# Weight splits held in order, the second pair's norms in later units, the last down products done plainly: one block of attention and GLU on one core

## The chip, the cores and the metric

The kernel runs on one core of a Trainium2 chip. The time is that of one execution on the device, in microseconds (us); the kernel before was run three times: 3179.58, 3184.73 and 3190.97, median 3184.73. PE is the matrix engine (TensorE), DVE the vector engine, ACT the scalar engine, POOL GpSimd, and SP the engine that issues all transfers (DMAs) here. Each engine runs its own instructions in order.

## The reference

All tensors are float32; S = 2048 rows, D = 576, 32 query heads over 16 key heads of 128, of whose cached 2048 keys the last W = 512 are used, and F = 4608.

```python
mod = (silu(c) @ w_mod).reshape(1, 6, 1, 576)
sa, ca, ga, sb, cb, gb = mod[:, 0], ..., mod[:, 5]
h = layernorm(x) * (1 + ca) + sa
q = (h @ wq) by heads; k, v = caches[:, :, Sk - W:], each for two query heads
x = x + ga * ((softmax(q @ k.T * 128**-0.5) @ v) by rows @ wo)
h = layernorm(x) * (1 + cb) + sb
x = x + gb * ((sigmoid(h @ w_gate) * (h @ w_up)) @ w_down)
```

## The kernel before

Products are made from split operands: a float32 number is a high part `hi` (a copy, rounded, made by ACT) and a low part `lo` (what is left, a subtraction on POOL or DVE), and `three` (L237) gives the three matmuls lo*hi, hi*lo, hi*hi.

The rows are four blocks of 512 in two halves: blocks 0 and 1 go through all heads first, then blocks 2 and 3, 128 (block, head) pairs, each in four steps (512 steps n). A step issues, in program order, a quarter of a coming query projection (`qproj`), the scores of step n + 2 (`scores`), the transposes of the probabilities (`transp`), one half of a row tile's output projection (`wo_acc`), a quarter of probabilities times values (`pv`) and the other half of `wo_acc`. The softmax of a step is a maximum on DVE (L354), an exponential on ACT (L356), four transposes on PE (L367) and two evictions (L370, L371).

What has to be made beside the steps is put in a table: `at_n(n, fn, ...)` calls fn at step n, in program order. wq is loaded 16 steps ahead of its use and split 8 ahead (`split_a`: ACT L207, POOL L208 and L209, four buffers wa), wo is loaded (L225), scaled by the gate (L420) and split (`split_b`: ACT L230, POOL L232, two buffers wb). Keys are loaded 15 steps ahead of their first step (L309) and transposed by PE 7 ahead (L315). The loads of wq, wo, keys and values share four buffers named raw.

The GLU of the second part is done by a seven-product scheme (Strassen-Winograd) over two halves of D, a pair of row blocks and pairs of F tiles. Its weights are prepared during attention as 135 *chunks*: each is loaded, summed, split and stored to DRAM (wsc for gate and up, dsc for down) while the other half's rows are at rest; the spare rows' buffers (x0, x1, or x2, x3) hold it. Chunk k starts at a step `n`, the next one three steps later, and takes its parts at fixed distances; sums alternate between two places by k, hi between two, raw between three. Chunks run from step 4 and, for the second part, from step 300 on. A chunk of kind tail is stored by 48 small DMAs (L648), the others by four or five (L654, L656).

A scheduler that goes by its own costs may move any instruction ahead of others on its engine, unless it is pinned: `keep_in_program_order` keeps pinned instructions in program order among themselves. The chunks are pinned and so is the copy in `split_b`; loads of raw and the splits of wq are not.

After attention, the second part runs 72 units u (pair of blocks, F tile). A unit makes the seven products (`product`, L849) of row combinations (hc, made by `load_combo` from transposed rows ts, loaded L723, transposed L736, split L737 and L739) with weights sw (L759); within each product two *down groups* (three matmuls, L241, and an addition to an accumulator in SBUF, L832 or L834) of the pair of F tiles before are done. A pair of units gives seven down values times four row tiles, 28 groups. After the last group of a pair of blocks, `finish` combines the accumulators by eight additions for each row tile and stores the output. The rows of the first pair are normed during attention (`early_norm`, `early_sums`); those of the second pair in units 0 to 2 (`late_stats`, then `late_tile`: L507 to L523), and the block buffers x2, x3 are parked in DRAM before (L536). The junction in what follows is the time from the last step of attention to the first full units, the pair switch is where blocks 2 and 3 take over.

## Time and profile before

| what | value |
|---|---|
| runs | 3179.58, 3184.73, 3190.97 us; median 3184.73 |
| profiled execution | 3187.44 us, its span 3185.7, granted clock 0.983 |
| PE busy | 3077.7 us, 17000 matmuls |
| DVE, ACT, POOL busy | 2173.0, 1444.2, 1555.8 us |
| DMA | 499.96 MB, mean 157 GB/s |
| attention | to 1880 us |
| junction | 1880 to 2000 us |
| GLU units | to 3150 us |
| last groups and stores | 3150 to 3186 us |

A row of the timeline reads: start, length, engine, line, operation, result <- operands, shape, count, and in brackets how long the engine stood idle just before and what ended it. The page's span is what one core did; the time on the device is 1.7 us longer.

### The profile page before, as it was taken

The page shows a single profiled execution, that of the slowest core. Times are in us where ns is not written, and L with a number is a line of the kernel's source. Part 1 is how long each engine was busy: PE and PEld are TensorE (multiplying, and loading weights), DVE is VectorE, ACT ScalarE, POOL GpSimd, SP SyncE. Part 2 cuts the span into 40 slices and gives each one's busy share as a digit, 9 for nine tenths or more (in the row PEclk, how much of TensorE's full clock was granted, in tenths as well). Part 3 has the DMA queues.
Part 4 walks back from the last instruction along what each step waited for, and adds up shares of the span by engine and source line. Part 5 has one row for each costly group of instructions (what it writes and reads, how often), then busy time and mean ns, then how long its engine had stood idle before and what let it go on. Part 6 is the DMA issues. An engine that isn't in the chain of part 4 may idle for free.

```text
span 3185.7 us, 50897 instructions
## 1 busy us (share of the span) xinstructions
PE 3077.7 (97%) x17000; PEld 2659.9 (83%) x17000; DVE 2173.0 (68%) x4214; ACT 1444.2 (45%) x3189; POOL 1555.8 (49%) x1925
## 2 busy tenths in 40 slices
PE   8999999999999999999999977999999999999998
PEld 6888887888888888888888866888888888888887
DVE  7777776777888777777777785555555665555556
ACT  5665655655554555656555532322222322222322
POOL 3656555664344335756565413433434353443435
PEclk8999999999999999999999988999999999999998
DMA  5556566555303235544444338766666776666663
GB/s 159 152 154 167 141 159 164 157 156 140 119 30 97 66 99 145 142 105 124 107 123 111 81 109 272 227 199 199 200 197 200 222 245 201 200 198 200 197 200 115
DMA packets 574437, 499.96 MB, mean 157 GB/s; under 512 B 191840, under 2 KB 455008, under 8 KB 573152
## 3 DMA queue, kind: packets, MB, share of 16 engines
q1 hardware_dynamic: 574176, 496.72, 54.4%
q8 instruction: 135, 2.21, 0.3%
q14 instruction: 126, 1.03, 0.1%
HBM read 356.35 MB, written 140.18 MB: 156 GB/s over the span
## 4 chain that ended last, share of the span: by engine, by line
PE 86%; POOL 4%; DVE 3%; DMA 3%; issue 2%; SPq 1%; ACT 1%; POOLq 0%; DVEq 0%; ACTq 0%
PE a L849 14%; PE w L241 12%; PE wo L241 11%; PE qp L241 11%; PE ot L241 10%; PE st L241 10%; PE c L849 7%; PE st L367 6%; PE b L849 3%; POOL x L637 1%; SPq L523 0%; PE w L736 0%; DMA ts<-scr 0%; DMA sw<-wsc 0%; DMA scr<-x 0%
## 5 line engine op out<-in xcount | busy, mean ns | idle before, releaser
L834 DVE TENSOR_TENSOR x<-w,x 128x288 f32<-128x288 f32 x976 | 443.2, 457 | 484.4 <-PE w L241 481.9
L241 PE MATMUL wo<-wb,ov 128*128 128x288 f32 x3072 | 623.1, 311 | 3.8 <-DVE ov L385 2.1
L241 PEld LDWEIGHTS w<-sd,hl 128*128 128x128 f32 x3024 | 515.0, 191 | 106.8 <-DVE x L832 12.1
L849 PE MATMUL a<-hc,sw 128*128 128x512 f32 x2016 | 582.4, 394 | 10.3 <-DVE hc L739 9.8
L241 PE MATMUL w<-sd,hl 128*128 128x288 f32 x3024 | 564.8, 297 | 20.5 <-DVE x L832 11.8
L370 ACT ACTIVATE ptt<-st 128x512 fp32r<-128x512 f32 x512 | 305.8, 597 | 606.5 <-PE st L367 605.9
L394 DVE SCALAR_TENSOR_TENSOR x<-wo,rs,x 128x288 f32<-128x288 f32 x1024 | 513.8, 512 | 55.7 <-PE wo L241 5.6
L354 DVE TENSOR_REDUCE neg<-st 128x1 f32<-128x512 f32 x512 | 352.6, 689 | 288.6 <-PE st L241 286.0
L241 PEld LDWEIGHTS wo<-wb,ov 128*128 128x128 f32 x3072 | 486.7, 190 | 56.0 <-DVE ov L385 4.9
L241 PE MATMUL qp<-hTm,wa 128*128 128x512 f32 x1536 | 445.5, 399 | 4.9 <-DVE qt L338 4.6
L241 PE MATMUL ot<-ptt,vs 128*128 128x512 f32 x1536 | 446.9, 399 | 0.0
L241 PE MATMUL st<-kt,qt 128*128 128x512 f32 x1536 | 440.1, 395 | 3.3 <-DVE ptt L371 3.2
L849 PEld LDWEIGHTS a<-hc,sw 128*128 128x128 f32 x2016 | 355.9, 188 | 49.4 <-DVE hc L739 10.3
L371 DVE TENSOR_TENSOR ptt<-st,ptt 128x512 fp32r<-128x512 f32 x512 | 348.7, 681 | 44.7 <-ACT ptt L370 44.4
L356 ACT ACTIVATE pp<-st,neg 128x512 f32<-128x512 f32 x512 | 350.4, 684 | 42.6 <-DVE neg L354 40.4
L241 PEld LDWEIGHTS st<-kt,qt 128*128 128x128 f32 x1536 | 289.0, 189 | 66.7 <-DVE ptt L371 3.9
L367 PEld LDWEIGHTS st<-ident,pp 128*128 128x128 f32 x2048 | 255.1, 140 | 97.9 <-ACT pp L356 30.8
L367 PE MATMUL st<-ident,pp 128*128 128x128 f32 x2048 | 308.8, 273 | 25.1 <-ACT pp L356 25.0
L849 PE MATMUL c<-hc,sw 128*128 128x512 f32 x1008 | 302.9, 395 | 7.0 <-DMA sw<-wsc 3.8
L637 POOL TENSOR_TENSOR x<-x,x 128x96 fp32r<-128x96 f32 (+3 forms) x364 | 228.3, 645 | 130.0 <-ACT x L632 126.4
L241 PEld LDWEIGHTS qp<-hTm,wa 128*128 128x128 f32 x1536 | 263.1, 190 | 31.5 <-DVE qt L338 5.6
L241 PEld LDWEIGHTS ot<-ptt,vs 128*128 128x128 f32 x1536 | 262.2, 190 | 23.6 <-DVE ptt L371 0.2
(140 smaller groups left out, 3710.8 us busy)
## 6 DMA issues: line engine op xcount, KB each, us to landing
sw<-wsc SPq DMA_DIRECT2D x504, 320.0 KB, 3.2
sd<-dsc SPq DMA_DIRECT2D x252, 288.0 KB, 2.8
wsc<-x SPq DMA_DIRECT2D x72, 448.0 KB, 3.4
raw<-in_A_wo_dram SPq DMA_DIRECT2D x64, 288.0 KB, 3.0
wsc<-x SPq DMA_DIRECT2D x72, 256.0 KB, 3.3
dsc<-x SPq DMA_DIRECT2D x54, 336.0 KB, 3.1
raw<-in_A_wq_dram SPq DMA_DIRECT2D x64, 256.0 KB, 3.0
dsc<-x SPq DMA_DIRECT2D x162, 96.0 KB, 2.5
```

What stands on the lines that cost most here:

```text
L241: nc.tensor.matmul(p, l, r, start=first and n == 0, stop=last and n == len(pairs) - 1)
L354: nc.vector.tensor_reduce(NEG[b][:, i : i + 1], p, axis=AX.X, op=OP.max, negate=True)
L356: nc.scalar.activation(PP[n], p, AF.Exp, bias=NEG[b][:, i : i + 1], accum_out=SUM[b][:, i : i + 1])
L367: nc.tensor.transpose(p[:, k * P : (k + 1) * P], PP[n][:, k * P : (k + 1) * P], ident)
L370: nc.scalar.activation(PT[b][:, 0, :, cols], pv_, AF.Copy)
L371: nc.vector.tensor_sub(PT[b][:, 1, :, cols], pv_, f32(PT[b][:, 0, :, cols]))
L394: nc.vector.scalar_tensor_tensor(xv, p, RS[b][:, i : i + 1], xv, op0=OP.mult, op1=OP.add)
L637: pin(nc.gpsimd.tensor_sub(v.bitcast(F32R), v, hi[:, a:b, :]))
L834: nc.vector.tensor_add(acc, p, acc)
L849: nc.tensor.matmul(p, l, r, start=first and n == 0, stop=n == len(pairs) - 1, skip_group_check=not first)
```

## The change

In attention, the high parts of wq and wo are pinned at their step, and the low parts become steps of their own two steps later, pinned too (so a raw buffer is freed later); wo's scaling is pinned. A chunk's sums come 3 steps after its load instead of 4, its copies 7 instead of 6, its subtractions 8 instead of 7 and its store 9 instead of 8. Then the rows: x2 and x3 are parked at the end of unit 0, after `late_stats`, which stands there now pinned; `late_tile` moves to units 4, 9, 14 and 19, reads the parked rows back into ts buffers and stores the seven combinations with 28 DMAs for a tile instead of 16. The loads of ts (`stage`) run two combinations ahead. At the end, the last pair of F tiles (group GL) is not summed by the seven-product scheme: its four values are multiplied by four of the eight plain quarter weights, 32 down groups instead of 28, as soon as each value is there, added to accumulators that the pair before (group 34) has already combined, in units 70 and 71 with three or six groups in a product. For that dsc of the last group has an eighth row.

```diff
-    def split_a(raw):
+    def split_a_hi(raw):
         sp = wp.tile([P, 2 * NC + 1, P], F32R, tag="wa", name="wa", bufs=4)
-        nc.scalar.activation(sp[:, : NC + 1, :], raw, AF.Copy)
-        nc.gpsimd.tensor_sub(sp[:, NC + 1 :, :], raw[:, :NC, :], f32(sp[:, :NC, :]))
-        nc.gpsimd.tensor_sub(sp[TAIL:, NC, :], raw[TAIL:, NC, :], f32(sp[TAIL:, NC, :]))
+        pin(nc.scalar.activation(sp[:, : NC + 1, :], raw, AF.Copy))
         return sp
+
+    def split_a_lo(raw, sp):
+        pin(nc.gpsimd.tensor_sub(sp[:, NC + 1 :, :], raw[:, :NC, :], f32(sp[:, :NC, :])))
+        pin(nc.gpsimd.tensor_sub(sp[TAIL:, NC, :], raw[TAIL:, NC, :], f32(sp[TAIL:, NC, :])))
...
     def scale_o(hh):
-        nc.gpsimd.tensor_mul(RB[hh], RB[hh], gate)
+        pin(nc.gpsimd.tensor_mul(RB[hh], RB[hh], gate))
...
         at_n(max(q_first(hh) - 8, NLO + 1), split_q, hh)
+        at_n(max(q_first(hh) - 6, NLO + 1), split_q_lo, hh)
...
         at_n(n, split_o, hh)
+        at_n(min(n + 2, o_first(hh) - 1), split_o_lo, hh)
...
-        at_n(n + 4, bg_sums, k)
-        at_n(n + 6, bg_hi, k)
-        at_n(n + 7, bg_lo, k)
-        at_n(n + 8, bg_store, k)
+        at_n(n + 3, bg_sums, k)
+        at_n(n + 7, bg_hi, k)
+        at_n(n + 8, bg_lo, k)
+        at_n(n + 9, bg_store, k)
...
-    for b in range(HB, NB):
-        park_x(b)
...
+    def late_tile(t):
+        lo, hi = slice(0, D2), slice(D2, D)
+        h0, h1, ts_ = [fh.tile([P, 2, D3], F32, tag="ts", name=n, bufs=3).rearrange("p a d -> p (a d)")[:, :D]
+                       for n in ("h0", "h1", "tt")]
+        for i, h in enumerate((h0, h1)):
+            nc.sync.dma_start(h, xscr[HB + i][:, t, :])
...
-        if u == 0:
-            late_stats()
-            late_tile(0)
-        if u == 1:
-            late_tile(1)
-            late_tile(2)
-        if u == 2:
-            late_tile(3)
-            init_acc(0)
...
+        if u in (4, 9, 14, 19):
+            late_tile((u - 4) // 5)
+        if u == NF - 2:
+            stage(1, 0)
...
+        downs = {U - 2: (0, 1, 2, 3, 4, 5), U - 1: (1, 3, 5)}.get(u, (2, 5))
...
+            if g == GL:
+                a, ops = (A11, ((0, A12), (7, S4))) if u % 2 else (A12, ((1, A12), (4, S4)))
+                VAL[g, a] = v
+                split_val(g, a)
+                todo += [(g, (a, o, to), t) for t in range(TPB) for o, to in ops]
```

**SP at a key load of the second run of chunks, near step 354** (raw_15798 and raw_15769 are those keys; raw_15841 and raw_15810 the wo rows that follow; dsc is a chunk's store; what a row waits for stands in brackets). Before:

```order
L202 DMA raw_15794<-in_A_wq_dram 64x128 [waits DMAHW5_49]
L309 DMA raw_15798<-in_A_k_cache_dram 128x512
L654 DMA dsc1_305<-x1_110 896x1x96 [waits DMAHW7_49,Activation_49]
L656 DMA dsc1_305<-x0_109 128x2x96 [waits DMAHW0_49,Pool_49]
L656 DMA dsc1_305<-x1_110 128x2x96 [waits DMAHW1_49,Pool_49]
L656 DMA dsc1_305<-x0_109 128x96 [waits DMAHW2_49,Pool_49]
L656 DMA dsc1_305<-x1_110 128x2x96 [waits DMAHW3_49,Pool_49]
L225 DMA raw_15841<-in_A_wo_dram 128x576 [waits DMAHW4_49]
L588 DMA x0_109<-in_B_w_down_dram 128x96 [waits DMAHW5_49,DMAHW0_49]
```

Now:

```order
L204 DMA raw_15765<-in_A_wq_dram 64x128 [waits DMAHW4_49]
L317 DMA raw_15769<-in_A_k_cache_dram 128x512
L232 DMA raw_15810<-in_A_wo_dram 128x576 [waits DMAHW6_49,DMAHW5_49,PE_49]
L670 DMA dsc1_305<-x1_110 128x7x96 [waits DMAHW7_49,Activation_49]
L672 DMA dsc1_305<-x0_109 128x2x96 [waits DMAHW0_49,Pool_49]
L672 DMA dsc1_305<-x0_109 128x2x96 [waits DMAHW1_49,Pool_49]
L672 DMA dsc1_305<-x0_109 128x96 [waits DMAHW2_49,Pool_49]
L672 DMA dsc1_305<-x0_109 128x2x96 [waits DMAHW3_49,Pool_49]
L602 DMA x0_109<-in_B_w_down_dram 128x96 [waits DMAHW4_49,DMAHW0_49]
```

The load of wo now stands ahead of the chunk's store, in the row behind the key load, and waits for PE: it reuses the buffer that holds those keys (the program's addresses of the two are the same).

**POOL and PE at the same place.** On POOL, now (x0 is the chunk's place; its first sum waits for a DMA, the store of two chunks before, and wa_15763 and wb_15771 are the low parts of wq and wo):

```order
L625 TENSOR_TENSOR x0_109<-x0_109 128x96 [waits DMAHW1_49,Pool_49]
L626 TENSOR_TENSOR x0_109<-x0_109 128x96 [waits Pool_49]
L627 TENSOR_TENSOR x0_109<-x0_109 128x96 [waits DMAHW3_49]
L628 TENSOR_TENSOR x0_109<-x0_109 128x96 [waits Pool_49]
L216 TENSOR_TENSOR wa_15763<-raw_15405,wa_15763 128x512
L217 TENSOR_TENSOR wa_15763<-raw_15405,wa_15763 64x128 [waits Pool_49]
L241 TENSOR_TENSOR wb_15771<-raw_15467,wb_15771 128x576 [waits PE_49,Pool_49]
```

PE before (st<-ident,raw are the key transposes, pp those of the probabilities):

```order
L367 MATMUL st_16116<-ident_69,pp_16033 128x128 x4
L241 MATMUL wo_16123<-wb_15800,ov_16085 128x288 x3
L241 MATMUL ot_16128<-ptt_15946,vs_15661 128x512 x3
L241 MATMUL wo_16132<-wb_15800,ov_16085 128x288 x3
L315 MATMUL st_16145<-ident_69,raw_15798 128x128 x4
L241 MATMUL qp_16166<-hTm_10987,wa_15790 128x512 x3
L241 MATMUL st_16170<-kt_15444,qt_15936 128x512 x3
L367 MATMUL st_16179<-ident_69,pp_16068 128x128 x4
```

PE now:

```order
L375 MATMUL st_16095<-ident_69,pp_16006 128x128 x4
L249 MATMUL ot_16107<-ptt_15918,vs_15634 128x512 x3
L323 MATMUL st_16122<-ident_69,raw_15769 128x128 x4
L249 MATMUL qp_16136<-hTm_10967,wa_15763 128x512
L249 MATMUL ot_16107<-ptt_15918,vs_15634 128x512 x2
L249 MATMUL st_16140<-kt_15414,qt_15908 128x512 x3
L375 MATMUL st_16149<-ident_69,pp_16040 128x128 x4
L249 MATMUL ot_16107<-ptt_15918,vs_15634 128x512 x2
L249 MATMUL st_16179<-kt_15414,qt_16084 128x512 x3
```

The wo groups of this step are gone from it (they stand four steps later, behind the query rows that read wa_15763), and only one query row is left before the subtractions.

**SP at the end of attention** (xscr2 and xscr3 are the parked rows of blocks 2 and 3). Before:

```order
L536 DMA xscr2_266<-x2_111 128x2304
L723 DMA ts_22716<-scr0_262 128x768
L536 DMA xscr3_267<-x3_112 128x2304
L759 DMA sw_22710<-wsc0_268 128x640
L759 DMA sw_22712<-wsc0_268 128x640
L759 DMA sw_22714<-wsc0_268 128x640
L723 DMA ts_22718<-scr0_262 128x768
```

Now:

```order
L553 DMA xscr2_266<-x2_111 128x2304
L736 DMA ts_22717<-scr0_262 128x768
L736 DMA ts_22719<-scr0_262 128x768
L736 DMA ts_22721<-scr0_262 128x768
L770 DMA sw_22777<-wsc0_268 128x640
L736 DMA ts_22723<-scr0_262 128x768
```

Three loads of ts stand right behind the parking of x2, and the parking of x3 is some 35 rows further on.

More of the change, by code (lines that the diff above doesn't have):

```diff
@@ L550, in adaln_block_kernel @@
     wsc = [dram.tile([P, 7, 5, P], F32, tag=f"wsc{f}", name=f"wsc{f}") for f in range(NF)]
-    dsc = [dram.tile([P, 7, 2, D2], F32, tag=f"dsc{g}", name=f"dsc{g}") for g in range(NF // 2)]
+    dsc = [dram.tile([P, 8, 2, D2], F32, tag=f"dsc{g}", name=f"dsc{g}") for g in range(NF // 2)]
     DW = D2 // 3
@@ L727, in load_combo @@
     def load_combo(pair, c):
-        if (pair, c) not in STG:
-            stage(pair, c)
         halves = STG.pop((pair, c))
@@ L771, in adaln_block_kernel @@
     x22 = bg_view(3, TPB * D2, [TPB, D2])
[L772 removed]
+    GL = 2 * NG - 1
+    sd_uses = [(g, a) for g in range(GL) for a in ORDER] + [(GL, i) for i in (0, 7, 1, 4)]
     at_sd = [0]
@@ L816, in finish, with down @@
         nc.gpsimd.tensor_add(c[S1], c[S1], c[S3])
-        for a, b, n0 in ((A12, b0, 0), (A22, b1, 0), (S4, b0, D2), (S1, b1, D2)):
-            nc.sync.dma_start(of[b][:, t, n0 : n0 + D2], c[a])
+        if pair == 0:
+            for a in (A12, A22, S4, S1):
+                store_out(a, pair, t)
+    def down(a, t, hl, w, fresh):
+        cols = slice(t * P, (t + 1) * P)
+        p = fpsum("w", 4, [P, D2])
+        mm_seq(p, three(hl[:, 0, cols], hl[:, 1, cols], w[:, 0, :], w[:, 1, :]))
+        acc = ACC[a][:, t, :]
+        if fresh:
+            nc.vector.tensor_copy(acc, p)
+        else:
+            nc.vector.tensor_add(acc, p, acc)
     def down_some(k):
@@ L950, in adaln_block_kernel @@
         nc.vector.tensor_mul(v1, v1, g1)
+        if u == 0:
+            late_stats()
         g = u // 2
-        if u % 2 == 0:
+        if g == GL:
+            a, ops = (A22, ((1, A22), (4, S1))) if u % 2 else (A21, ((0, A22), (7, S1)))
+            VAL[g, a] = v1
+            split_val(g, a)
+            todo += [(g, (a, o, to), t) for t in range(TPB) for o, to in ops]
+        elif u % 2 == 0:
             VAL[g, A21] = v1
```

138 lines of the change are left out of this document (84 added, 54 removed).

## The prediction

> **What bounds the kernel now.** I read the page first, then PE's waits, then busy time by stage, then single stretches. The page:
>
> ```profile
> PE 3077.7 (97%) x17000; PEld 2659.9 (83%) x17000; DVE 2173.0 (68%) x4214; ACT 1444.2 (45%) x3189; POOL 1555.8 (49%) x1925
> ```
>
> PE (TensorE) is busy 97% of the span, so an edit pays only where PE stands, or where it runs at a lower granted clock. PE's waits, largest first:
>
> ```profile
> PE st L367 <- ACT pp L356: 25.0, 11, 4.7
> PE w L241 <- DVE x L832: 11.8, 1, 11.8
> PE w L736 <- DMA ts<-scr: 11.8, 5, 8.5
> PE a L849 <- DVE hc L739: 9.8, 1, 9.8
> ...
> PE w L241 <- POOL hl L791: 4.7, 5, 1.7
> ...
> PE c L849 <- DMA sw<-wsc: 3.8, 1, 3.8
> ...
> PE st L241 <- DVE ptt L371: 3.2, 1, 3.2
> ```
>
> Columns: total us, times, longest. The next view is busy time by window (start:end, length, PE, PEld, DVE, ACT, POOL, granted clock, DMA share, GB/s; x counts instructions):
>
> ```profile
> 1100.00:1200.00 100.00, 100.00 (x573) 86.63 (x572) 75.79 (x140) 56.36 (x129) 38.77 (x55) 1.00 0.38 99
> 500.00:600.00 100.00, 94.48 (x521) 80.54 (x520) 68.20 (x126) 54.87 (x128) 54.47 (x78) 0.97 0.58 151
> 700.00:800.00 100.00, 96.74 (x543) 83.20 (x542) 71.67 (x132) 57.02 (x133) 58.31 (x85) 0.98 0.56 147
> 1300.00:1400.00 100.00, 96.86 (x545) 83.37 (x544) 71.92 (x132) 58.14 (x145) 64.41 (x112) 0.98 0.46 117
> 1500.00:1600.00 100.00, 96.87 (x544) 83.44 (x543) 72.63 (x134) 56.34 (x144) 57.05 (x101) 0.98 0.41 105
> 1600.00:1700.00 100.00, 97.18 (x546) 83.55 (x545) 71.76 (x131) 57.41 (x147) 66.84 (x120) 0.98 0.49 127
> 1880.00:1900.00 20.00, 1.95 (x7) 1.55 (x8) 15.65 (x45) 1.57 (x3) 10.15 (x8) 0.55 0.66 236
> 1900.00:1920.00 20.00, 18.60 (x106) 14.77 (x105) 10.97 (x18) 11.26 (x20) 0.00 (x0) 0.94 0.81 255
> 1920.00:1940.00 20.00, 15.39 (x68) 12.05 (x67) 12.77 (x17) 5.57 (x11) 8.79 (x7) 0.92 0.88 268
> 1940.00:1960.00 20.00, 8.15 (x37) 6.60 (x36) 10.07 (x13) 4.94 (x9) 15.88 (x12) 0.76 0.69 190
> 1960.00:1980.00 20.00, 18.34 (x89) 16.10 (x89) 8.36 (x18) 4.17 (x7) 3.81 (x3) 0.90 0.86 266
> 1980.00:2000.00 20.00, 19.45 (x97) 16.70 (x97) 10.12 (x22) 5.77 (x10) 8.51 (x7) 0.91 0.91 329
> 2600.00:2700.00 100.00, 100.00 (x543) 87.55 (x542) 56.21 (x114) 29.63 (x51) 41.91 (x33) 1.00 0.68 206
> 3150.00:3186.00 36.00, 21.25 (x102) 17.75 (x100) 24.91 (x52) 2.82 (x5) 25.04 (x24) 0.76 0.25 82
> ```
>
> Undisturbed attention does 573 matmuls in 100 us, the GLU 543. Three places lose time. Attention windows fall short by counts: 521, 543, 545, 544 and 546 against 573 are 9.1 + 5.2 + 4.9 + 5.1 + 4.7 = 29 us. The junction (1880 to 2000) is PE-busy 81.9 of 120 us, 38.1 idle; multiplying each busy time by the missing clock adds 8.8, so 47. The last 36 us hold 102 matmuls, 19 us of work at the GLU's rate.
>
> **The change part by part.** *Attention stalls removed.* POOL, ACT and PE around 1520 us:
>
> ```profile
> 1506.71 1.30 POOL L208 TENSOR_TENSOR wa<-raw,wa 128x512 fp32r<-128x512 f32 x1 [7.50 <-ACT wa L207]
> 1508.09 0.47 POOL L209 TENSOR_TENSOR wa<-raw,wa 64x128 fp32r<-64x128 f32 x1
> 1509.62 1.42 POOL L232 TENSOR_TENSOR wb<-raw,wb 128x576 fp32r<-128x576 f32 x1 [1.07 <-ACT wb L230]
> ```
> ```profile
> 1519.82 0.36 ACT L632 ACTIVATE x<-x 128x192 fp32r<-128x192 f32 x1 [2.33 <-POOL x L609]
> 1521.30 0.36 ACT L632 ACTIVATE x<-x 128x192 fp32r<-128x192 f32 x1 [1.12 <-POOL x L612]
> ```
> ```profile
> 1522.87 0.66 PE L367 MATMUL st<-ident,pp 128*128 128x128 f32 x4 [2.81 <-ACT pp L356]
> ```
>
> POOL stood 7.50 us at wq's subtraction, the chunk's sums came late, ACT's copies of them (L632) waited 2.33 and 1.12, the exponentials (L356) were queued behind, and PE stood 2.81. The change puts four steps instead of two between sums and copies and holds wq's subtraction two steps behind its copy. So I take the 29 us as removed. ACT's wait for wq's load goes too, with the 3.2 us at L371 above:
>
> ```profile
> 816.94 0.74 ACT L207 ACTIVATE wa<-raw 128x640 fp32r<-128x640 f32 x1 [4.28 <-DMA raw<-in_A_wq_dram]
> ```
>
> A second such wait is within the 25.0; together 6. Removed: 35 us.
>
> *Attention stalls added.* The four weight buffers are now freed two steps later, and the first pair of orders shows wo's load reusing the buffer of the key load right ahead of it: SP stands until PE has transposed those keys, with the chunk's stores queued behind. Key load and transposes are eight steps apart in the table; a step is 19.5 matmuls, 3.4 us at 573 per 100, so SP can stand 27 us. SP's own issues, outside chunk work, show such a hold, there for another reader of a raw buffer:
>
> ```profile
> 874.34 0.42 SPq L225 DMA_DIRECT2D raw<-in_A_wo_dram  x1
> 876.60 0.33 SPq L309 DMA_DIRECT2D raw<-in_A_v_cache_dram  x1
> 905.09 0.38 SPq L200 DMA_DIRECT2D raw<-in_A_wq_dram  x1
> ```
>
> No chunk runs in that stretch, so nothing pinned stood behind it. Now the store's landing releases the sums of two chunks later, and behind those POOL holds, pinned, the subtractions of wq and wo which PE's wo and query groups read. PE's new order says the same: the wo groups stand four to five steps later there. The stores' price:
>
> ```profile
> 1394.02 0.56 SPq L654 DMA_DIRECT2D dsc<-x  x1
> 1394.68 2.44 SPq L656 DMA_DIRECT2D dsc<-x  x4
> ```
> ```profile
> dsc<-x SPq DMA_DIRECT2D x162, 96.0 KB, 2.5
> ```
>
> From the transposes: wo's issue 0.4, stores 0.56 + 2.44, landing 2.5, four sums at about 0.4, then 1.30 + 0.47 + 1.42: 10.7 us. PE meanwhile has scores, transposes and values of four steps, 10 of 19.5 matmuls each: 4 x 3.4 x 10/19.5 = 7.0. It loses 3.7, and I add 1.3 for half clock afterwards: 5.0. The order shows seven such places, 48 steps apart in two runs (steps 42, 90, 138, 186; 362, 410, 458): 35 us. One of them runs into a store of many pieces:
>
> ```profile
> L648 SPq DMA_DIRECT2D wsc<-x x432: 302/427/1744, 162.9 to 1264.7; - x144
> ```
>
> Nine stores, 48 issues each, 427 ns: 20.5 us of SP. Behind the block at step 42 the next landing comes that much later; SP has 10.3 - 3.0 = 7.3 us free in the three steps between two chunks, so 13 more. A second such store at step 154, less hemmed in, I put at 5, lateness behind two others at 4 each, and small irregular places in PE's order at 2. Added: 63 us. Bounds: 25, if only the seven lose their bare 3.7; 110, if each place loses what it waits without cover, 10.7, and the rest 35.
>
> What the half clock adds is seen in two windows just after a stall:
>
> ```profile
> 1523.70:1527.10 3.40, 3.07 (x10) 2.70 (x10) 2.77 (x6) 1.78 (x5) 3.24 (x8) 0.50 0.64 163
> 815.80:819.20 3.40, 0.27 (x1) 0.27 (x2) 1.01 (x2) 2.26 (x6) 1.32 (x2) 1.00 0.00 0
> ```
>
> After 2.81 us idle the clock was 0.50 for 3.4 us, a loss of about 1.5; through an idle 3.2 it stayed 1.00. [...]
>
> *Junction.* The shared-row loads (ts) no longer stand behind the store of x3, the statistics of the second half go to the end of unit 0, its norms to units 4, 9, 14 and 19. This removes what stood behind the 8.5 (ts), 9.8 (DVE at the norms) and 11.8 (the first accumulator copy, DVE) with their half clock; the 3.8 at sw stays, as that load follows the same transfers. A bound is transfers: fourteen ts of 393 KB, seven sw of 328 KB and a parked block of 1.2 MB before unit 0 can end, 9 MB, 30 us at the 300 GB/s between the rows. They start where the first ts does now,
>
> ```profile
> 1868.62 1.77 SPq L723 DMA_DIRECT2D ts<-scr  x1
> ```
>
> some 11 us before PE's work runs out at 1880, so 19 us of unit 0 remain against about 12 of work (six products and the transposes). Of 47 I take 28 off; bounds 10 (only ts) and 40. The moved norms put some 9 us of POOL on each of four units of 16.7 us, where POOL is 42% busy (9.7 free): covered; without cover, 3 each. Each moved tile also issues 30 DMAs instead of 16 from SP, at 427 ns 13 us within a unit whose 14 weight loads (seven sw, seven sd) take 6 more: SP is more than full there for a unit, and that is one reason to stay 12 below the 40.
>
> *Pair switch and tail.* Earlier ts at the second pair: 3. The last product but one ends here:
>
> ```profile
> 3149.36 0.39 PE L849 MATMUL a<-hc,sw 128*128 128x512 f32 x1
> ```
>
> 36 us follow, with 28 down groups and the additions that combine them. Now group 34 is finished within unit 70 and the last pair uses 32 plain groups, about half of them behind that point: a product 1.6, the last value split 2.6, groups at DVE's 0.46 and the store, 15 us. Earlier PE work is 60 matmuls more (0.13 each, 8), and DVE's combination in unit 70 costs 4: 36 - 15 - 8 - 4 = 9; bounds 2 and 15.
>
> **Sum.** -35 + 63 - 28 - 3 - 9 = -12. The profiled execution took 3187.4 (span 3185.7), so 3175.4; it lay 2.7 above the median 3184.7: forecast 3173.
>
> **Rivals.** *No new attention stalls:* the weights wait only on paper, since chip durations run shorter than the scheduler's. For it: the order of before was regular and yet stalled elsewhere, so order is no clock. Against: SP's wait is in the instruction, and 27 us of it were seen. With 0 added, 3184.7 - 75 = 3110; with 30, 3140.
>
> *Slower: SP held behind the key buffer.* One mechanism, at the seven places: SP issues nothing until the keys are transposed, and PE then runs without wo and query work. It decides from 85 us added (35 + 40 + 10), which is 8.0 per place with the other 28. At 9 each, 3200; at the bare 10.7, 3212. For it: the softmax chain may stretch PE's four steps. Against: PE has 7.0 of cover. [...]
>
> *No change:* the junction gives 10 because transfers, 329 GB/s at the end of the rows, take the stalls' place: 3191; with the other terms a little better, 3180.
>
> **How the numbers follow.** Forecast 0.43 (its own range 3140 to 3174), no new stalls 0.12, slower 0.26, no change 0.19. About 0.3%, 9.6 us, can be told from nothing. Faster is 0.43 + 0.12 = 0.55, same 0.19, slower 0.26. The range 3132 to 3212 leaves out about 0.08 below and 0.1 above, most of the first rival's bare case and the slower one's compounding.
>
> **What would show it.** Right: the L367 waits at 1349, 1520 and 1691 are gone; instead idle PE with SP standing 25 us or more at wo's load near steps 42, 90, 362; ts landing before attention ends; PE over 17 busy of 20 us from 1900. Wrong: SP never over 15 us at wo's load while chunks run (first rival), or PE idle over 8 us per place (second), or a junction still at 300 GB/s with PE idle (third).

## The result, and the profile after

The change makes the kernel slower: 3258.48 us (median of four, 3255.18 to 3262.8) against 3187.39 for the kernel before in the same runs, a ratio of 1.0227 with an interval of 1.0203 to 1.0251. The forecast was 3173 and the range ended at 3212.

The page of the changed kernel, its first row:

```profile
PE 3124.2 (96%) x17012; PEld 2677.0 (82%) x17012; DVE 2167.5 (66%) x4202; ACT 1449.4 (44%) x3189; POOL 1561.6 (48%) x1937
```

PE is busy 46 us longer for 12 matmuls more, so time is lost inside its busy time too. PE's waits now:

```profile
PE st L375 <- ACT pp L364: 24.0, 15, 4.4
PE qp L249 <- POOL wa L216: 19.2, 11, 3.5
PE wo L249 <- POOL wb L241: 13.5, 15, 1.5
PE c L873 <- ACT v L880: 12.1, 4, 6.1
...
PE w L747 <- DMA ts<-scr: 5.6, 5, 1.9
```

The second and third rows are new: PE's query and wo groups wait for the low parts that POOL makes of wq and wo. The first row is hardly smaller than before (25.0): its waits now lie elsewhere, most of them in the first half of attention. The long waits of the junction (11.8, 11.8 and 9.8) are gone; one of 6.1 us, in the fourth row, is new there.

Where the 75 us between the two profiled spans (3261.0 and 3185.7) arose is seen best by comparing the same work in both timelines: the start of a step's first transpose, and of a unit's second product.

| place | before, us | after, us | later by | since the row above |
|---|---|---|---|---|
| step 9 | 77.0 | 88.9 | 11.9 | +11.9 |
| step 45 | 202.3 | 225.0 | 22.7 | +10.8 |
| step 63 | 265.5 | 306.1 | 40.6 | +17.9 |
| step 126 | 487.4 | 557.9 | 70.5 | +29.9 |
| step 216 | 812.5 | 915.8 | 103.2 | +32.7 |
| step 297 | 1117.1 | 1218.2 | 101.1 | -2.1 |
| step 504 | 1847.7 | 1945.3 | 97.6 | -3.5 |
| unit 4 | 1994.3 | 2061.9 | 67.6 | -30.0 |
| unit 24 | 2330.3 | 2406.8 | 76.5 | +8.9 |
| unit 60 | 2952.8 | 3034.2 | 81.4 | +4.9 |
| unit 71 | 3137.6 | 3227.8 | 90.3 | +8.9 |
| end | 3185.7 | 3261.0 | 75.4 | -14.9 |

The GLU gains 22. Attention loses 98, nearly all of it in the first run of chunks (steps 4 to 220); in the second run (from step 300) the change even gains a little. The stretch from step 18 to step 216, before and then after (columns as before):

```profile
107.90:812.50 704.60, 693.81 (x3922) 598.15 (x3921) 520.46 (x959) 423.14 (x984) 417.81 (x595) 0.99 0.59 156
```
```profile
119.90:915.80 795.90, 731.55 (x3923) 614.72 (x3921) 521.15 (x957) 425.60 (x986) 411.33 (x590) 0.95 0.51 137
```

Of these 91 us PE stands idle for 54 more, and 38 are busy time that became longer for the same matmuls, with the granted clock at 0.95 instead of 0.99. In smaller windows of the change:

```profile
200.00:300.00 100.00, 86.51 (x435) 69.65 (x434) 58.41 (x107) 50.79 (x118) 54.98 (x78) 0.91 0.55 144
300.00:400.00 100.00, 91.09 (x492) 77.81 (x491) 64.39 (x121) 54.41 (x127) 54.04 (x77) 0.95 0.55 147
...
1200.00:1300.00 100.00, 100.00 (x574) 86.68 (x573) 75.97 (x141) 56.11 (x128) 34.59 (x46) 1.00 0.33 86
...
1980.00:2000.00 20.00, 16.74 (x90) 13.10 (x91) 9.59 (x15) 10.08 (x18) 0.00 (x0) 0.91 0.86 277
2000.00:2020.00 20.00, 18.23 (x92) 14.73 (x91) 17.30 (x51) 7.47 (x14) 3.81 (x3) 1.00 1.02 387
2020.00:2040.00 20.00, 13.94 (x57) 11.32 (x57) 14.29 (x24) 5.77 (x10) 10.02 (x8) 0.83 0.67 234
```

Between 200 and 300 us PE did 435 matmuls where undisturbed it does 573. The first of the foreseen places (step 42) lies there. SP, PE and POOL:

```profile
168.03 0.34 SPq L612 DMA_DIRECT2D x<-in_B_w_up_dram  x1
203.04 0.33 SPq L232 DMA_DIRECT2D raw<-in_A_wo_dram  x1
203.46 0.52 SPq L670 DMA_DIRECT2D wsc<-x  x1
204.04 2.36 SPq L672 DMA_DIRECT2D wsc<-x  x3
```
```profile
202.41 0.60 PE L323 MATMUL st<-ident,raw 128*128 128x128 f32 x4
...
211.83 0.80 PE L249 MATMUL qp<-hTm,wa 128*128 128x512 f32 x1 [1.98 <-POOL wa L216]
```
```profile
208.73 0.45 POOL L631 TENSOR_TENSOR x<-x 128x128 f32<-128x128 f32 x1 [33.24 <-issue]
...
210.51 1.26 POOL L216 TENSOR_TENSOR wa<-raw,wa 128x512 fp32r<-128x512 f32 x1
...
212.38 1.41 POOL L241 TENSOR_TENSOR wb<-raw,wb 128x576 fp32r<-128x576 f32 x1
...
238.38 0.46 POOL L631 TENSOR_TENSOR x<-x 128x128 f32<-128x128 f32 x1 [22.26 <-DMA wsc<-x]
```

SP issues nothing from 168.4 to 203.0, until PE has transposed the keys; then come wo's load, the store, its landing, the sums and the low parts, 203.0 to 213.8: 10.8 us, and the prediction's chain had 10.7. But 25 us later POOL has stood another 22.26 for the next store, one of 48 pieces (a *large store* in what follows), and from there on it is that which repeats.

### The profile page after: what moved, and what is told of

Its sections match the earlier page's. It is cut to its first block, busy times and chain, and to the rows that moved or that the text cites. A ratio compares the mean times of both kernels' runs of the same rounds, so it can differ in the third digit from the quotient of the medians.

```text
span 3261.0 us, 50848 instructions
## 1 busy us (share of the span) xinstructions
PE 3124.2 (96%) x17012; PEld 2677.0 (82%) x17012; DVE 2167.5 (66%) x4202; ACT 1449.4 (44%) x3189; POOL 1561.6 (48%) x1937
## 4 chain that ended last, share of the span: by engine, by line
PE 53%; DMA 2%; POOL 2%; DVE 2%; SPq 1%; issue 1%; ACT 0%; POOLq 0%; DVEq 0%; ACTq 0%
PE a L873 13%; PE w L249 11%; PE c L873 7%; PE wo L249 5%; PE qp L249 4%; PE ot L249 4%; PE st L249 3%; PE b L873 3%; PE st L375 2%; DMA ts<-scr 1%; SPq L663 1%; DMA wsc<-x 0%; PE w L747 0%; DVE x L845 0%; POOL hl L804 0%
## 5 line engine op out<-in xcount | busy, mean ns | idle before, releaser
L249 PE MATMUL wo<-wb,ov 128*128 128x288 f32 x3072 | 623.6, 314 | 19.7 <-POOL wb L241 13.5
L249 PEld LDWEIGHTS wo<-wb,ov 128*128 128x128 f32 x3072 | 493.5, 194 | 78.9 <-POOL wb L241 20.8
L249 PE MATMUL qp<-hTm,wa 128*128 128x512 f32 x1536 | 464.2, 408 | 30.0 <-POOL wa L216 19.2
L375 PEld LDWEIGHTS st<-ident,pp 128*128 128x128 f32 x2048 | 254.8, 141 | 106.9 <-ACT pp L364 35.6
L375 PE MATMUL st<-ident,pp 128*128 128x128 f32 x2048 | 312.8, 275 | 26.6 <-ACT pp L364 24.0
L652 POOL TENSOR_TENSOR x<-x,x 128x96 fp32r<-128x96 f32 (+4 forms) x367 | 229.2, 645 | 64.3 <-ACT x L647 64.1
```

Source lines behind the costliest of these rows:

```text
L249: nc.tensor.matmul(p, l, r, start=first and n == 0, stop=last and n == len(pairs) - 1)
L375: nc.tensor.transpose(p[:, k * P : (k + 1) * P], PP[n][:, k * P : (k + 1) * P], ident)
L652: pin(nc.gpsimd.tensor_sub(v.bitcast(F32R), v, hi[:, a:b, :]))
```

## The experiments

Kernels of a group ran on the same chip beside the kernel before (3183 to 3185). In the tables "pause at wo" is what SP paused before wo's loads (L232) between steps 18 and 216, pauses over 1 us summed, and in brackets the longest (kernel before: 16.2, 8.0); "at 216" is how much later than in the kernel before step 216 begins.

### One part undone at a time

The first kernel has the second part of the change alone. Its edits, and what the other three take of them (it also has, as the kernel before, one chunk more in the first run and one less in the second: 71 and 64, where the change has 70 and 65):

```diff
# old distances (second kernel, and first)
-        at_n(n + 3, bg_sums, k)
-        at_n(n + 7, bg_hi, k)
-        at_n(n + 8, bg_lo, k)
-        at_n(n + 9, bg_store, k)
+        at_n(n + 4, bg_sums, k)
+        at_n(n + 6, bg_hi, k)
+        at_n(n + 7, bg_lo, k)
+        at_n(n + 8, bg_store, k)
# low parts at once (fourth kernel, third and first)
-        at_n(max(q_first(hh) - 6, NLO + 1), split_q_lo, hh)
+        at_n(max(q_first(hh) - 8, NLO + 1), split_q_lo, hh)
-        at_n(min(n + 2, o_first(hh) - 1), split_o_lo, hh)
+        at_n(n, split_o_lo, hh)
# not pinned (third kernel, and first): wq's parts, wo's low part, wo's scaling
-        pin(nc.gpsimd.tensor_sub(sp[:, 1, :], raw, f32(sp[:, 0, :])))
+        nc.gpsimd.tensor_sub(sp[:, 1, :], raw, f32(sp[:, 0, :]))
```

> The change's second part alone (parking, statistics, norms, ts loads, last pair), with the attention of before: splits not held, distances 4, 6, 7, 8. By the stage-by-stage comparison of the two traces the second part gained 22 us (junction 30, late norms -9, pair switch -3, end 6, rest -2), and attention lost 98. If the two add up: 3187 - 22 = 3165, within 6. If the first part's order changes what the second gains (the transfers at the junction start from another place), it lies outside 3155 to 3175.

> All of the change but the four distances, which are 4, 6, 7, 8 as before; splits stay pinned and their low parts two steps later. Theory A (a chunk's sums now stand at the step of the store of two chunks before, so POOL waits for that store to land, 20 us for a store of 48 pieces, with the pinned low parts behind it): the loss in the first run of chunks goes, the stalls of ACT's copies come back in part: 3165 to 3195. Theory B (the pins alone do it) or theory C (raw buffers freed two steps later, SP held at wo's load): at least 3230.

> All of the change but the splits: as before they are not pinned (only wo's copy is) and both parts stand at one step; distances 3, 7, 8, 9 stay. Theory A in its narrow form (POOL's wait at the sums hurts whatever is behind): POOL still waits some 20 us at each of the nine large stores, and at least 40 us of the loss stay, 3215 or more. Theory B (what hurts is that the low parts are held behind the waiting sums): POOL may wait, PE does not, 3155 to 3185.

> All of the change, but the low parts of wq and wo at the step of their high parts, still pinned, so that the raw buffers come free as before; distances 3, 7, 8, 9. Theory C (late raw buffers, SP held at wo's load behind the key load): 3155 to 3200. Theory A with the pins as its means: POOL still waits for the large stores and the low parts are still pinned, though two steps earlier: about half of the loss or more stays, 3215 to 3258.

| kernel | us | ratio to before | pause at wo, us | at 216 |
|---|---|---|---|---|
| the change | 3258.5 | 1.0227 (1.0203 to 1.0251) | 113.3 (34.7) | +103.2 |
| second part only | 3155.8 | 0.9903 (0.9887 to 0.9920) | 18.2 (8.4) | +0.9 |
| old distances | 3155.7 | 0.9906 (0.9892 to 0.9921) | 63.0 (14.1) | +1.9 |
| splits free | 3140.3 | 0.9857 (0.9842 to 0.9871) | 12.2 (4.8) | -2.1 |
| low parts at once | 3152.1 | 0.9894 (0.9880 to 0.9909) | 36.6 (8.6) | +12.5 |

Undoing any one of the three takes the whole loss away, 102.8 to 118.2 us. Each came out a little below what the theory that spoke for it had said, and that all three did so at once shows that none of the three is the cause by itself. It is not POOL's waiting for the large stores as such either. POOL's waits at the sums, of the change and then of the kernel with low parts at once, which is 12.5 us late at step 216 and loses nothing over all:

```profile
POOL x L631 <- DMA wsc<-x: 295.6, 48, 23.7
```
```profile
POOL x L631 <- DMA wsc<-x: 246.0, 45, 23.6
```

What the four fast kernels share is that SP has no long pause at wo's load (none over 14.1 us, where the change has 34.7). They share one thing more: PE's order is regular in them. In the change 51 of 512 steps have their wo groups elsewhere (counted in the trace, between the first transposes of one step and of the next), in these four none. The second part alone came out at 3156, 9 us better than the sum of the traces had said (3165) and just inside the range that went with it; the pair switch and the units around it lost less there.

With the splits free, the stalls at ACT's copies that the new distances were to remove are gone and little comes in their place: by the same comparison of steps it gains 9.0 and 5.0 at the two places in the first run and 5.3, 4.1 and 4.8 at the three in the second. The prediction had 9.1, 5.2, 4.9, 5.1 and 4.7. (At step 126 this kernel is 11.5 us late, at 216 2.1 ahead.)

### The hold taken away, and the landing

Two theories were left. C: SP's hold at wo's load is the cause. L: a large store lands 20 to 24 us late on POOL, more than the steps that a low part has until it is used.

```diff
# first: keys and values in a buffer of their own
-        raw = raw_tile([P, KT, DH])
+        raw = wp.tile([P, KT, DH], F32, tag="kvraw", name="kvraw", bufs=1)
-            at_n(n - 10, load_v, gg)
+            at_n(n - 6, load_v, gg)
# second: sums behind a large store three steps later
-        at_n(n + 3, bg_sums, k)
+        at_n(n + (6 if k > 1 and jobs[k - 2][0] == "tail" else 3), bg_sums, k)
# third: low parts one step later than the high parts (q_first - 7, n + 1); fourth: only wq's two steps later
```

> All of the change, but keys and values are loaded into one buffer of their own (values 6 steps ahead instead of 10), so that no load of wo can wait for the keys' transposes. Distances, pins and late low parts stay. Theory C (SP held at wo's load behind the key load, 170 us in all, which makes every store behind it late): 3145 to 3180. Theory L (the landing of a large store, 20 to 24 us on POOL, against the 17 us that a low part of wo has now until it is used, 24 with the low part at once): the nine large stores still cost some 7 to 10 us each, 3215 to 3258.

> All of the change, but the sums of the chunk that comes two after a large store (48 pieces) start 6 steps after its load instead of 3, so that they are due three steps, 10 us, after that store and not at its step; the hold at the key load stays. Theory L: POOL's longest wait at the sums falls from 24 to about 13 us, under the 17 of slack, and 40 to 70 us of the loss go: 3185 to 3215. Theory C: 3235 to 3260.

> All of the change, but the low parts one step after the high parts instead of two (with none it was 3152). Theory L: the slack is 20.6 us against waits of up to 24, so a part of the loss: 3165 to 3200. Theory C: the raw buffers come free between the two, and what counts is whether a wo load meets the key buffer: either end, 3150 to 3160 or above 3230, by the order of the loads.

> All of the change, but wo's low part at once; only wq's stays two steps later. Theory L: wo has its 24 us again, wq keeps 20.6 instead of 27: a part of the loss at most, 3160 to 3200. Theory C: the buffers of wq are freed late, and wo's loads wait for PE in even more places in the order of the program (24 against 21): 3220 or more.

| kernel | us | ratio to before | pause at wo, us | at 216 |
|---|---|---|---|---|
| keys in their own buffer | 3161.0 | 0.9924 (0.9909 to 0.9940) | none | +22.8 |
| sums behind large stores later | 3240.2 | 1.0164 (1.0145 to 1.0183) | 110.2 (34.7) | +88.5 |
| low parts one step later | 3171.3 | 0.9954 (0.9938 to 0.9970) | 53.0 (6.0) | +32.3 |
| only wq's low part late | 3152.8 | 0.9896 (0.9881 to 0.9910) | 33.2 (8.8) | +13.2 |

The first run decides between the two: with distances, pins and late low parts all as in the change, a buffer that takes the hold away brings 97 us. PE's order is regular with it again, so what share of the 97 that order has is not settled here. L explains a smaller part, 18 us where POOL's wait is shortened (its longest fell from 23.7 to 19.0, not to the 13 expected); it may explain the 13 to 32 us that the three fast kernels here are still late at step 216, which was not shown. The third run lies where L had put it, at neither end that C had named. The last missed L's 3160 from below, and by far what C had said from the number of waits in the program's order (24 such rows against 21): in these runs the number of rows told nothing, the length of the wait did. SP's wait for PE at wo's load over the whole program (total, times, longest), in the change, with sums later, and with low parts one step later:

```profile
SPq L232 <- PE st L323: 170.0, 12, 35.0
```
```profile
SPq L232 <- PE st L323: 168.7, 12, 35.0
```
```profile
SPq L232 <- PE st L323: 27.5, 6, 8.4
```

### Is it SP's time?

In the change, SP's issues between steps 18 and 216 take 463 of 796 us, pauses under 4 us 182, and longer ones 150 (summed over SP's rows); in the kernel before 483, 179 and 41 of 705. In the second run (steps 300 to 500) the change has 360 of 703 us of issues, and there holds of 22, 35 and 34 us cost some 3 us each. (That run differs in its work too: only two of the nine large stores fall into it, both ahead of these holds.) Theory S: SP is nearly full in the first run, so time taken from it is time of the program. Theory O: what costs is the order of PE that the scheduler made round the hold (the 51 irregular steps).

```diff
# 32 pieces: the seven high parts go together
                 for to in range(4):
-                    for a, b, lo in bg_pairs(k):
-                        src = lo if to % 2 else hi[:, a:b, :]
+                    for a, b, src in (bg_pairs(k) if to % 2 else [(0, 7, hi)]):
                         pin(nc.sync.dma_start(wsc[f + q][to * TQ : (to + 1) * TQ, a:b, 4, :], src[rows]))
# more issues: behind each large store
+            for j in range(48):
+                pin(nc.sync.dma_start(spare[j], w_gate[j : j + TQ, :P]))
```

> All of the change, with the large stores in 32 pieces instead of 48 (the seven high parts of a row group lie side by side and go in one transfer instead of three); the hold at the key load and the irregular order of PE stay. Theory S (in the first run of chunks SP is nearly full: 58% issuing, 23% in waits under 4 us, so each us that it is held there is a us of the program; in the second run, 51% issuing, the same hold costs nothing): 7 large stores x 16 issues x 0.43 = 48 us of SP are taken away, and 30 to 50 us of the loss with them: 3208 to 3230. Theory O (the order of PE that the scheduler chose round the holds is what costs): at most 15 us, 3243 or more.

> The kernel with free splits (3140), with 48 more DMAs behind each large store, which copy some rows of a weight to a place nobody reads: SP's issues alone, 20.5 us each time, 7 x 20.5 = 144 us between steps 18 and 216, against 150 us of long holds in the change. Nothing waits for a key buffer and no split is pinned. Theory S: SP was at 67% and 28% in short waits there; 50 to 110 us longer, 3190 to 3250. If the loss needs the hold at the key load or the pins: 3140 to 3160.

> The kernel with free splits (3140) and the large stores in 32 pieces. Theory S: SP is not the bound there any more, so what is left to win is POOL's wait for the landing, 17 instead of 24 us: 3130 to 3141. Otherwise the same, 3140.

> As the one before, with keys and values in a buffer of their own, so that wq and wo have four raw buffers to themselves. With all holds of raw loads gone the splits come earlier: 3125 to 3140; if the scheduler places them by their use anyway, the same as the one before.

| kernel | us | ratio to before | pause at wo, us | at 216 |
|---|---|---|---|---|
| the change, store of 32 | 3235.3 | 1.0162 (1.0147 to 1.0177) | 135.0 (34.7) | +85.3 |
| splits free, 48 more issues | 3317.2 | 1.0417 (1.0401 to 1.0432) | 1.3 (1.3) | +142.7 |
| splits free, store of 32 | 3134.0 | 0.9840 (0.9826 to 0.9855) | 15.9 (4.8) | -6.2 |
| the same, keys in their own buffer | 3133.4 | 0.9841 (0.9823 to 0.9858) | 22.0 (14.6) | -5.3 |

The smaller store brings 23 us, between what S and what O had said. Its waits for PE at wo's load grew by 24 us, since a hold lasts until PE is at the keys and SP was there earlier:

```profile
SPq L232 <- PE st L323: 194.0, 12, 35.0
```

The issues saved are fewer than the 48 us expected: in the first run the large stores take 114.7 us of issues instead of 148.5, since the joined pieces take longer (the median of one is the middle number, in ns):

```profile
L662 SPq DMA_DIRECT2D wsc<-x x288: 303/452/1798, 208.3 to 1359.3; - x144
```

So 34 us of issues less stand against 22 of pause at wo more, and step 216 came 18 earlier.

The other way round, the 48 issues more behind each large store, without a hold at wo or a pinned split, made step 216 145 us later than in their own base (142.7 against -2.1) and the program 177 us longer. They were not the 144 us expected, but 202 between steps 18 and 216, since these copies take longer to issue:

```profile
L666 SPq DMA_DIRECT2D spare<-in_B_w_gate_dram x432: 488/589/1511, 193.0 to 1477.6; - x144
```

The 177 lie above the 50 to 110 that S had said; measured by their own length, 145 of 202 is 0.72, which S's 50 to 110 of 144 take in. So the first run has little to spare on SP. But PE's order became irregular too, at 71 steps, so O is not excluded by it.

The last two are the fastest kernels of this study: 1.6% faster than before, with the second part of the change, the new distances, the splits as before and the large stores in 32 pieces.

### The same hold at another load

To have a hold without the irregular order, keys and values share one buffer (as above) and the values are loaded ten steps ahead again, so that SP stands at their load until the keys are transposed.

```diff
-        raw = raw_tile([P, KT, DH])
+        raw = wp.tile([P, KT, DH], F32, tag="kvraw", name="kvraw", bufs=1)
```

> The change with keys and values in one buffer of their own (3161 with the values 6 steps ahead), but the values again loaded 10 steps ahead, so that SP stands at their load for three steps, some 10 us, until PE has transposed the keys: 12 such holds, 125 us, between steps 18 and 216 (the change: 4 holds, 79 us). PE's order is regular except at 13 steps. Theory S (SP nearly full, a hold costs its own length once the free time is used): 3200 to 3280. Theory O (the irregular order of PE cost the time): 3161 to 3180.

> The same holds at the values' load, with the splits free (without holds 3140, or 3133 with smaller stores). Theory S in its strong form (SP alone): 3185 to 3260. Theory SP (the hold reaches PE only through low parts that stand pinned behind waiting sums): 3135 to 3165.

> The same holds, with the splits pinned and late, and the four distances of before (without holds 3156). Theory S in its strong form: 3200 to 3270. If the new distances are needed (sums at the step of the store before them): 3156 to 3180.

| kernel with the hold | us | ratio to before | kernel beside it |
|---|---|---|---|
| all of the change | 3197.7 | 1.0043 (1.0026 to 1.0059) | 3161.0 |
| splits free | 3164.2 | 0.9934 (0.9919 to 0.9948) | 3140.3 |
| old distances, splits pinned and late | 3150.6 | 0.9892 (0.9877 to 0.9907) | 3155.7 |

The kernels beside them are the change with keys and values in their own buffer, with splits free, and with old distances. Only the first is the same kernel without the hold; the other two have four shared raw buffers and values ten steps ahead. SP's wait at that load over the whole program, and POOL's at the sums, first for all of the change, then for the old distances:

```profile
SPq L317 <- PE st L323: 141.9, 23, 19.8
```
```profile
POOL x L631 <- DMA wsc<-x: 258.3, 41, 24.6
```
```profile
SPq L317 <- PE st L323: 126.9, 22, 17.2
```
```profile
POOL x L631 <- DMA wsc<-x: 130.3, 17, 19.5
```

Most of these totals lie behind the first run. Between steps 18 and 216, SP's pauses at the values' load came to 30.0, 4.6 and 37.4 us and not to 125, since SP is late there and finds the keys transposed. (The irregular steps of the first kernel are 18 in the trace, not 13.) Read with that:

- With all of the change, 30 us of hold make step 216 22.8 us later than the same kernel without them (+45.6 against +22.8). By step 126 there were 22.1 us of hold and 15.5 of loss, and the first irregular step is 128: so here it is the hold and not PE's order that costs.
- The change's own pauses at wo, 113 us, made step 216 80 us later (103.2 against 22.8).
- So long pauses cost about 0.7 of their length with the new distances: 16 of 22 and 23 of 30 here, 80 of 113 with the irregular order, and 145 of 202 for issues instead of a hold. Short ones cost less: with low parts one step later they are 53.0 us, none over 6.0, and step 216 is at +32.3.
- With the old distances pauses cost nothing that can be seen: 37.4 us at the values' load with step 216 at -6.3, and in the kernel beside it 63.0 us at wo's load (most of it, 38.4 us, until POOL has made wq's low part, L217) with step 216 at +1.9, although SP issues 497 and 502 of some 700 us there.

S in its strong form falls, as SP's time alone does not decide: it takes the new distances. For the change itself the share of PE's irregular order was not separated from the hold. The run with free splits tells little: it lost 24 us with 4.6 us of pauses at the values' load in the first run, and what else the shared buffer delays there was not followed up.

### Which of the distances

A chunk k + 2 writes its sums where chunk k had them, so they wait for the store of k to land. With the new distances POOL has, at one place of the program, the sums of k + 2 *ahead of* the subtractions of k + 1, for which the store of k + 1 waits; with the old ones it has them behind. Theory R: in the new order store, landing, sums, subtractions and next store form a ring through SP and POOL with one chunk in it. Its time by the rows above: from the store's first issue to the first sum 5.3 (203.46 to 208.73), sums 4 x 0.45, subtractions 2.4, together 9.5; with the low parts, 1.3 + 0.45 + 1.4, where they fall in between, 12.7. A chunk is due every 10.3. Such a ring wins back little or nothing of what it lost to a hold or to a store of 24 us.

```diff
-        at_n(n + 3, bg_sums, k)
+        at_n(n + 5, bg_sums, k)
```

(n + 4 in the second kernel; the third has free splits and the store of 32.)

> The kernel with the hold at the values' load and all of the change (3198; without the hold 3161), sums 5 steps after the load instead of 3: on POOL a chunk's subtractions now stand ahead of the sums of the next chunk instead of behind them. Theory R (with the new distances POOL does sums of chunk k + 2, which wait for the store of k to land, before the subtractions of k + 1, which the store of k + 1 waits for: a ring through SP and POOL with one chunk in it, that cannot win back a hold): the ring is open, the holds cost nothing as with the old distances: 3148 to 3168. If only SP's time counts: 3185 or more.

> The same with sums 4 steps after the load: one step more between store and sums, but on POOL the sums still stand ahead of the subtractions of the chunk before. Theory R: the ring stays closed, 3180 to 3200. If each step of distance counts for itself (slack between store and sums): half of the loss, 3168 to 3182.

> The fastest kernel so far (free splits, large stores in 32 pieces, 3134) with sums 5 steps after the load, so that the ring is open there too. Theory R: no hold is left to win back, so 3125 to 3136; if the two steps taken from the way between sums and copies bring ACT's waits back (2.8 us of PE each, 5 places in the kernel before): 3136 to 3150.

| kernel | us | ratio to before | was |
|---|---|---|---|
| hold at the values' load, sums at 5 | 3169.1 | 0.9954 (0.9939 to 0.9969) | 3197.7 at 3 |
| the same, sums at 4 | 3187.1 | 1.0015 (1.0005 to 1.0024) | 3197.7 at 3 |
| splits free, store of 32, sums at 5 | 3163.3 | 0.9938 (0.9921 to 0.9956) | 3134.0 at 3 |

One step of distance brings 10.6 us, the second, with which the order turns, 18.0. At 5, step 216 is 3.3 us late instead of 45.6, at 4 27.3, with pauses of 21.8 and 27.8 us at the values' load. That is R's way (the first 1 us above its bound, the second within), but one step of distance counts too, so the ring is supported and not shown alone. The third run missed: the two steps taken from the way between sums and copies cost 29 us, not 2 to 16. PE's waits, first at 5 and then at 3 steps, account for 13.5 of them (the profiled execution at 5 was the fastest of its four, 3153.3):

```profile
PE st L375 <- ACT pp L364: 23.8, 13, 4.1
```
```profile
PE st L375 <- ACT pp L364: 10.3, 10, 2.4
```

So the new distance between sums and copies is worth having, where nothing holds SP.

## Why the prediction was wrong

**The attention stalls removed, 35.** Right in kind and size where they can be seen alone: with free splits the five places give 28 us against 29 foreseen. In the change the waits at steps 364, 412 and 460 are gone as well, the sign that had been named. But PE's total at L375 stayed (24.0 against 25.0), since such waits appeared at other steps of the first half (2.84 at step 6, 2.78 at 22; 4.4 at 216, where ACT's copies of sums stood 4.02 until a late store had landed).

**The attention stalls added, 63.** This is the step that failed. Attention got 98 us longer with 35 taken off, so about 133 were added, above the bound of 110. By its parts:

- The large stores: "13 more" for one, 5 for a second and 4 for two others, 26 in all, rested on the sentence that SP has 7.3 us free between two chunks, so that lateness is made good before the next store. It is not: six of the seven stores of the first run were followed by losses of 17.9, 11.1, 9.6, 7.7, 11.5 and 9.3 us (steps 45 to 63, 72 to 81, 99 to 117, 117 to 135, 153 to 162, 207 to 216), 67 together. I looked at SP's free time within one chunk, and not at what the new order on POOL does to it. This is the largest miss.
- The start: 12 us by step 9, which I had at nothing. SP loads keys and values only when POOL's low part of wq has freed a raw buffer (62.6 us), ACT's copy of the values (L331) waits 2.88 us for their landing, and PE then waits 1.89 and 2.84 for ACT's exponentials (steps 4 and 6). POOL's wait for the gate (10.1 us at L431) does not decide: with keys and values in their own buffer it is the same, and step 9 is only 2.9 late.
- The seven places at a key load, 5 each: in the second run they come to about 3 (net -2.4, -0.5 and -1.9 where free splits gain 5.3, 4.1 and 4.8), in the first to 6.2 and 8.9 at steps 42 and 90 and, with the stalls removed there added back, some 6 and 8 at 138 and 186. Together about 38 against 35. The chain of one place, 10.8 us against 10.7, was right. SP stood 34.7, 18.8 and 22.1 us at steps 40, 88 and 360, and 35.0 and 33.8 at 408 and 456, where the sign named was 25 or more.
- The half clock, in the sum 1.3 at each of the seven places: the longer busy time of the first run, 38 us, is counted within the items above. Most of it is the clock: 0.04 less of 796 us are an estimated 32.

**The junction, 28.** Right: 30 by unit 4. The first three loads of ts landed by 1974.3, ahead of attention's last matmul at 1976.9, as foreseen. The transfers peaked at 387 GB/s in the window from 2000 to 2020, but over the three windows shown they made 299, so the bound of 300 held. PE was over 17 of 20 us busy in the second of the three windows alone.

**The late norms, nothing (3 each without cover).** 8.9 us by unit 24, 2 each: the cover was not whole.

**Pair switch, 3 gained.** About 3 lost, and some 2 more up to unit 60. With the second part alone it gained 0.8; what differs is open.

**The end, 9.** 6: 8.9 more before the last unit (8 foreseen), 14.9 won behind it (17 foreseen, 36 - 15 - 4). In unit 71 one matmul of the second product was drawn ahead of its place; measured at the last matmul of the product before it (3137.4 and 3230.0) the two are 11.2 and 17.2.

**The rivals.** The slower one had the mechanism, SP held behind the key buffer, with 0.26, and its top price, 3212 at 10.7 per place, was 46 us short for the same reason: it multiplied places and did not ask whether SP and POOL recover between them. Its total, over 85 us added, came true; the way it was to come, PE idle over 8 us at each of the seven places, did not: PE's longest single wait between step 0 and the end of attention was 4.4. No new stalls and no change fell with the result.

**Where half clock came.** After idle times of 1.98 us, ended at 211.8, and of 0.72 and 1.06 us, ended at 1615.2 and 1618.0, the windows show a granted clock of 0.50 (first and third row; the second, with most of the 1.98, is at 1.00):

```profile
211.80:218.60 6.80, 6.41 (x20) 5.20 (x21) 1.55 (x3) 0.28 (x2) 4.20 (x5) 0.50 0.17 34
207.00:211.80 4.80, 2.83 (x13) 1.66 (x11) 3.17 (x5) 3.87 (x9) 2.97 (x5) 1.00 0.60 158
1618.10:1621.50 3.40, 3.40 (x13) 3.12 (x14) 1.03 (x2) 0.00 (x0) 3.32 (x7) 0.50 0.40 101
```

So it was not only the 2.81 us of the prediction: shorter stalls were followed by half clock too.

**What stays open.** That the ring on SP and POOL is what keeps the first run from recovering is supported by the old distances and by sums at 5, but sums at 5 also give two steps of slack. Every kernel that is over 80 us late at step 216 has PE's irregular order as well, at 45 to 71 steps, and it was never run by itself; in the second run it stands at three places and costs, with holds of 22, 35 and 34 us, some 3 us at each. The 24 us that the shared buffer cost with free splits, and the 5 us between units 24 and 60, were not explained.

## What to carry to other kernels

Before an operation is held in order, look at what it then frees later, and at which load takes that buffer next: two steps more for a low part moved a wait for PE, up to 35.0 us long, into SP's queue, with everything that SP issues behind it. When due times of a pipelined chore are shifted, compare not only its own stages but the order of *neighbouring* items on the engine they share; a stage of the next item that moves ahead of a stage of the last one can close a ring, and a ring as long as its period has no time to recover (here supported, not shown alone). And a sum of local stalls is right only where the engine that is delayed has time to catch up: take its share over the whole stretch first.

## What the runs showed of the hardware

Issuing was a cost of the first order here. A store of 48 small transfers held SP 23 to 29 us, each issue 0.43 us by the median, and a piece landed 1.6 us after its issue, by the median too (1.4 to 4.0); over the first run of the kernel before SP issued in 68% of the time (483 of 705 us). The issues stood one behind the other, 48 x 0.43 = 20.5 us; the landings overlapped, for 48 of 1.6 one after the other would be 77. Joining them to 32 took POOL's longest wait for a store from 13.2 us to 7.9 with free splits, first row and second, and 6 us off the time:

```profile
POOL x L631 <- DMA wsc<-x: 123.9, 41, 13.2
```
```profile
POOL x L631 <- DMA wsc<-x: 90.7, 39, 7.9
```

The length of a gap alone did not tell whether half clock followed. In the change a gap of 1.98 us, ended at 211.8, was followed by 6.8 us at a granted clock of 0.50 (the first row of the windows in the section on the prediction). In the kernel before, a gap of 3.16 us, ended at 818.9, passed at 1.00, and so did the 6.8 us behind it:

```profile
815.80:818.90 3.10, 0.00 (x0) 0.00 (x0) 0.71 (x2) 1.96 (x5) 1.10 (x1) 1.00 0.01 0
818.93:825.73 6.80, 6.80 (x39) 5.94 (x40) 5.79 (x12) 4.40 (x11) 6.30 (x9) 1.00 0.69 207
```

What else decided was not shown.
